# The normalized rows of a spectral block get a tile of their own: a third slot for the tag of the transfer tile

## The chip, the cores and the metric

The kernel runs on one core of one Trainium2 chip. The metric is the device time of one execution in microseconds (us), the median over several runs. Engines are named as the profile names them: PE (matrix products), PEld (its weight loads), DVE (VectorE), ACT (ScalarE), POOL (GpSimd) and SP, whose queue issues every DMA of this kernel ("SPq").

## The reference

Eight sequences x of 3136 rows and 256 channels pass through a spectral layer and then through a Fourier mixer with an MLP. Cut to what is computed:

```python
X = rfft(x, axis=1)
Yr = Xr @ w_r - Xi @ w_i + b_r
Yi = Xr @ w_i + Xi @ w_r + b_i
Y = soft(Yr) + 1j * soft(Yi)          # soft(v) = sign(v) * max(|v| - 0.01, 0)
y = irfft(Y, n=3136, axis=1)          # the "x" of the second part
u = y + real(fft(fft(y, axis=1), axis=2))
un = (u - mean(u)) / sqrt(var(u) + 1e-6)     # over the 256 channels
out = u + relu(un @ w_ch1) @ w_ch2    # 256 -> 1024 -> 256
```

## The kernel before, in words

A sequence of 3136 = 64 x 49 rows is transformed in two stages: first over the 64 (p1), then over the 49 with the twiddles in a table (p2_f2). p2_w mixes the channels and applies the soft threshold. From its result two things are made: the inverse transform (p2_yt transposes, p2_g2 does its first stage and stores it to the DRAM tensor bd), and the mixer's part, for which the spectrum is already there (p2_mix; its DVE, ACT and POOL steps end in the tile mq, stored to the DRAM tensor md). Most products are made in three terms of a high and a low part (mm3, lines L150, L151, L152); a tile ending in h is the high part and one ending in l the low part, and the lo helpers (L144 on DVE, L147 on POOL) make the latter.

The part around the change is p3, which runs over *pieces*: two of the 49 columns of a sequence at once, or one (there are 104 pieces, and 12 or 14 belong to a batch, that is a sequence; three or four columns make a group). For each piece:

- p3_norm loads a tile bf from bd (L669) and a tile mt from md (L673 and L675, three or six DMAs to a piece's rows), both from SP. ACT and POOL split bf into bh and bl, PE does the last stage of the inverse transform (g_g1), and DVE adds it to mt, which gives u in the tile ut (L683). DVE, ACT and POOL make mean and reciprocal deviation (L688 to L698), and L700 writes the normalized rows, **in place into mt**.
- p3_tr transposes them on PE (g_ut, L718); ACT and DVE make the two parts uth and utl.
- p3_mlp1 makes h = un @ w1 on PE in eight slices; ACT makes hh with the relu (L737) and DVE hl (L738). p3_mlp2 multiplies with w2 into o; DVE adds ut (L757) and SP stores the rows (L759).

Tiles come from a pool by tag. A tag has a number of slots (bufs), and a new tile takes the next one; the framework makes its first writer wait until all readers of the tile that held it are done. The tag of mt is also used by the split of the weights at the start (split_double, its tiles tf and r), by wi and by inv_f. The tile im (L445, L446) holds the imaginary part in one of the ways in which p2_f2 takes a result out of PSUM.

The order of the instructions on each engine is fixed when the program is built. Every step of each batch is a generator that yields a due time, and a heap takes the earliest; the pieces of p3 are due at

```python
yield t0 + T3 * (NRM + i / 4)      # p3_norm
yield t0 + T3 * (TR + i / 4)       # p3_tr
yield t0 + T3 * f / 8              # p3_mlp1
```

On top of that the framework orders the instructions with a time line of its own (`TileContext(nc, schedule_with_timeline_sim=True)`), in which an instruction is placed once its slots are there. So slots are handed out in the program's order, and a load whose slot is still held stands back in SP's row. At run time each engine's row is worked off from front to back. Other DMAs in SP's row are xf and ad (p1), af and tff (p2_f2's load and its table), tif (p2_yt's table), bd and md stores (L642; L565 to L579), and the stores to the output.

Of the kernel before, what the change touches and what calls it, by code (L numbers as in the profile page):

```python
# [10 lines left out]
F32 = mybir.dt.float32  # L11
# [8 lines left out]
D = 256  # L20
# [6 lines left out]
S = 50  # L27
# [101 lines left out]
def spectral_block(ctx: ExitStack, tc: tile.TileContext, x, w_ri, b_ri, w1, w2,  # L129
# [28 lines left out]
    def split_double(name, h, l, sl, src):  # L158
# [3 lines left out]
        def tmp(tag, bufs, dt=I32):  # L162
            return sb.tile([128, 512], dt, tag=tag, bufs=bufs, name=f"cv_{name}_{tag}")
# [3 lines left out]
        lo, hi = raw[:, 0::2], raw[:, 1::2]  # L167
        tf = tmp("mt", 2, F32)
        sc.activation(tf, hi.bitcast(F32), AF.Abs)
# [8 lines left out]
        va.tensor_scalar(e, w, -0x800000, None, op0=ALU.bitwise_and)  # L178
        r = tmp("mt", 2)
        va.tensor_scalar(r, lo, 8, None, op0=ALU.logical_shift_right)  # L180
# [24 lines left out]
    def load_consts():  # L205
        yield 0.97 * T
        behind("x", out=fwd_f, in_=c_fwd)
        w_v = w_ri.rearrange("a (k p) e -> a p k e", p=128)
        for name, tag in (("wr", "hh"), ("ws", "hh"), ("wd", "hl")):
            KF[name] = sb.tile([128, 2, D], F32, tag=tag, bufs=2, name=name + "f")  # L210
        behind("x", out=KF["wr"], in_=w_v[0])
        wi = sb.tile([128, 2, D], F32, tag="mt", bufs=2, name="wi")
        behind("x", out=wi, in_=w_v[1])

        for name, sign in (("ws", -1.0), ("wd", 1.0)):
            va.scalar_tensor_tensor(KF[name], wi, sign, KF["wr"], op0=ALU.mult, op1=ALU.subtract)
        for name in ("wr", "ws", "wd"):
            split(name, KF[name])
        yield 0.99 * T
        KF["cs"] = sb.tile([128, 2, 129], F32, tag="hl", bufs=2, name="csf")  # L220
        behind("x", out=KF["cs"], in_=c_cs)
        yield 1.55 * T
        split("fwd", fwd_f)

        cs = K["cs"] = cp.tile([128, 2, 2, 128], F32R, name="cs")
        t = KF["cs"]
        sc.copy(cs[:, :, 0], t[:, :, 0:128])
        lo_v(cs[:, :, 1], t[:, :, 0:128], cs[:, :, 0])
        sc.copy(cs[:, 0, 1, 0:1], t[:, 0, 128:129])
        inv = sb.tile([128, 128], F32, tag="mt", bufs=2, name="inv_f")  # L230
        nc.sync.dma_start(out=inv, in_=c_inv)
        split("inv", inv)
# [157 lines left out]
    def p2_f2(b):  # L390


        for q in range(4):
# [17 lines left out]
            for ui in range(4):  # L411
# [30 lines left out]
                else:  # L442
                    im = sb.tile([128, 2, 2, S], F32, tag="im", bufs=2, name="im")
                    put(sc.copy, [Xh], gv)
# [209 lines left out]
    def p3_norm(b):  # L654

        for gi, (g0, z) in enumerate(groups[b % 2]):
            t0, T3 = clock3(b, g0)
            for i, n in parts_of[z]:
# [7 lines left out]
                bf = sb.tile([128, 512], F32, tag="bf", bufs=2, name="bf")  # L666
                mt = sb.tile([128, 2, D], F32, tag="mt", bufs=2, name="mt")
                for r, (bb, n2) in enumerate(src):
# [28 lines left out]
                gp.tensor_scalar(vv[:, :n], vv[:, :n], -0.5, 1.5, op0=ALU.mult, op1=ALU.add)  # L697
                gp.tensor_mul(rs[:, :n], rs[:, :n], vv[:, :n])  # L698
                for j in range(n):
                    va.tensor_scalar(mt[:, j], ut[:, j], ag[:, j, 0:1], rs[:, j], op0=ALU.subtract, op1=ALU.mult)  # L700
                normed[b, gi, i] = mt
                uts[b, gi, i] = ut

    def p3_tr(b):
        for gi, (g0, z) in enumerate(groups[b % 2]):
            t0, T3 = clock3(b, g0)
            for i, n in parts_of[z]:
                yield t0 + T3 * (TR + i / 4)
                if i == 0:
                    uth = sb.tile([128, 2, 512], F32R, tag="uth", bufs=2, name="uth")  # L710
                    utl = sb.tile([128, 2, 512], F32R, tag="utl", bufs=2, name="utl")
                    uthl[b, gi] = uth, utl
                mt = normed.pop((b, gi, i))
                g = gtile("g_ut")
                gv = g.rearrange("p (k t) -> p k t", k=2)
                for j in range(n):
                    for k in range(2):
                        te.transpose(gv[:, k, j * 128:(j + 1) * 128], mt[:, j, k * 128:(k + 1) * 128], ident)  # L718
                tw = slice(i * 128, i * 128 + n * 128)
# [103 lines left out]
```

## Time and profile before

| | |
|---|---|
| median of 3 runs | 1958.12 us (1956.15 to 1961.05) |
| the profiled execution | 1961.45 us |
| its span, from first to last instruction | 1959.7 us |
| mean granted clock of PE | 0.969 |
| PE, PEld busy | 95%, 87% of the span |
| DVE, ACT, POOL busy | 67%, 44%, 36% |
| DMA | 233.05 MB, 119 GB/s |
| chain that ended last | PE 80%, DVE 7%, DMA 6%, SP's queue 3% |

The median is over unprofiled runs; every duration and wait in the text is from the one profiled execution. A timeline row gives start and length in us, engine, line, operation, tile written and tiles read, and in brackets how long the engine had been idle and what ended that. A row of a DMA on SPq shows how long SP took to issue it, not the transfer. A row of the view of waits reads: engine and line that waited, engine and line waited for, us in total, times, longest.

### The profile page before, as it was taken

To read this page: it belongs to the slowest core of one execution; us is meant where nothing else is said; L and a number is where in the kernel's file an instruction comes from. 1 tells how busy PE (TensorE), PEld (TensorE's weight loads), DVE (VectorE), ACT (ScalarE), POOL (GpSimd) and SP (SyncE) were. 2 spreads that over 40 slices of the span, in tenths; PEclk is the share of its full clock that TensorE was granted. 3 is DMA by queue.
4 is the path that set the end of the run, shared out by engine and by line. 5 is a ranking of instruction groups with operands and counts; after the bars stand their busy time and mean duration, and the time that the engine had idled before them with its cause. 6 is when DMAs were issued, how large, how long until landed. Compare 5 with 4: busy or idle time off the path is not lost.

```text
span 1959.7 us, 35047 instructions
## 1 busy us (share of the span) xinstructions
PE 1856.2 (95%) x12115; PEld 1709.1 (87%) x12115; DVE 1322.5 (67%) x2831; ACT 853.2 (44%) x1888; POOL 704.8 (36%) x1087
## 2 busy tenths in 40 slices
PE   4875799999999999999999999999999999999999
PEld 3764699989999999998999999998999998998999
DVE  2676677777776777766677777766777766675543
ACT  2443544444444454443444544434544434433322
POOL 0345544344433444343333443323543322322210
PEclk7886899999999999999999999999999999999999
DMA  7466654345443544434443444435433332223210
GB/s 215 122 177 192 154 139 131 101 119 148 115 122 109 152 129 121 117 98 138 136 134 104 136 137 114 127 99 141 136 106 98 107 98 89 83 70 109 68 41 25
DMA packets 163540, 233.05 MB, mean 119 GB/s; under 512 B 27484, under 2 KB 107428, under 8 KB 163364
## 3 DMA queue, kind: packets, MB, share of 16 engines
q1 hardware_dynamic: 163364, 230.82, 41.9%
q8 instruction: 97, 1.59, 0.3%
q14 instruction: 79, 0.65, 0.1%
HBM read 127.95 MB, written 102.76 MB: 118 GB/s over the span
## 4 chain that ended last, share of the span: by engine, by line
PE 80%; DVE 7%; DMA 6%; SPq 3%; issue 2%; ACT 1%; POOL 1%; DVEq 0%; POOLq 0%; ACTq 0%
PE o L150 8%; PE o L151 8%; PE o L152 8%; PE h L150 8%; PE h L151 8%; PE h L152 8%; PE g_f L419 4%; PE g_w L150 3%; PE g_w L152 3%; PE g_w L151 3%; PE g_g L150 2%; PE g_g L152 2%; PE g_g L151 2%; PE g_yt L609 2%; PE g_ut L718 2%
## 5 line engine op out<-in xcount | busy, mean ns | idle before, releaser
L151 PE MATMUL o<-w2h,hl 128*128 128x256 f32 x1568 | 431.4, 285 | 8.4 <-DVE hl L738 8.4
L738 DVE SCALAR_TENSOR_TENSOR hl<-h,hh 128x512 fp32r<-128x512 f32 (+1 forms) x416 | 272.3, 655 | 243.8 <-ACT hh L737 242.5
L737 ACT ACTIVATE hh<-h 128x512 fp32r<-128x512 f32 (+1 forms) x416 | 238.0, 573 | 443.0 <-PE h L152 382.7
L152 PE MATMUL o<-w2h,hh 128*128 128x256 f32 x1568 | 424.2, 280 | 0.0
L150 PE MATMUL o<-w2l,hh 128*128 128x256 f32 x1568 | 397.6, 286 | 2.5 <-DVE ut L757 2.3
L150 PE MATMUL h<-utl,w1h 128*128 128x512 f32 (+1 forms) x832 | 323.5, 389 | 8.1 <-DVE hl L738 8.1
L152 PE MATMUL h<-uth,w1h 128*128 128x512 f32 (+1 forms) x832 | 317.0, 381 | 0.0
L151 PE MATMUL h<-uth,w1l 128*128 128x512 f32 (+1 forms) x832 | 316.6, 381 | 0.0
L151 PEld LDWEIGHTS o<-w2h,hl 128*128 128x128 f32 x1568 | 297.3, 190 | 14.8 <-DVE hl L738 10.3
L152 PEld LDWEIGHTS o<-w2h,hh 128*128 128x128 f32 x1568 | 297.0, 189 | 3.2
L150 PEld LDWEIGHTS o<-w2l,hh 128*128 128x128 f32 x1568 | 286.3, 189 | 15.1 <-ACT Xsh L428 2.9
L147 POOL TENSOR_TENSOR bl<-bf,bh 128x512 fp32r<-128x512 f32 x104 | 130.0, 1251 | 298.3 <-ACT bh L678 296.1
L419 PE MATMUL g_f<-tff,af 98*128 98x100 f32 x1024 | 155.2, 284 | 25.8 <-DMA tff<-c_tf 13.0
L419 PEld LDWEIGHTS g_f<-tff,af 98*128 98x128 f32 x1024 | 148.5, 204 | 34.2 <-issue 23.4
L152 PEld LDWEIGHTS h<-uth,w1h 128*128 128x128 f32 x832 | 156.8, 189 | 23.8
L150 PEld LDWEIGHTS h<-utl,w1h 128*128 128x128 f32 x832 | 157.0, 189 | 22.8 <-DVE hl L738 9.0
L147 POOL TENSOR_TENSOR xl<-xf,xh 128x512 fp32r<-128x512 f32 (+1 forms) x75 | 97.1, 1295 | 203.2 <-ACT xh L362 201.3
L151 PEld LDWEIGHTS h<-uth,w1l 128*128 128x128 f32 x832 | 157.3, 189 | 13.4
L683 DVE TENSOR_TENSOR ut<-g_g,mt 128x512 f32<-128x512 f32 x104 | 68.3, 657 | 104.9 <-PE g_g L152 67.9
L147 POOL TENSOR_TENSOR Xl<-xx,Xh 128x400 fp32r<-128x400 f32 (+1 forms) x96 | 106.3, 1110 | 89.6 <-ACT Xh L428 69.3
L147 POOL TENSOR_TENSOR Xsl<-xs,Xsh 128x200 fp32r<-128x200 f32 x120 | 76.9, 642 | 161.4 <-ACT Xsh L428 144.2
L700 DVE TENSOR_SCALAR mt<-ut,ag,rs 128x256 f32<-128x256 f32 x196 | 90.8, 502 | 48.9 <-POOL rs L698 48.6
(155 smaller groups left out, 3811.3 us busy)
## 6 DMA issues: line engine op xcount, KB each, us to landing
bd<-bev SPq DMA_DIRECT2D x128, 196.0 KB
af<-ad SPq DMA_DIRECT2D x62, 392.0 KB
bf<-bd SPq DMA_DIRECT2D x184, 128.0 KB
out_dram<-ut SPq DMA_DIRECT2D x92, 256.0 KB
xf<-in_x SPq DMA_DIRECT2D x176, 128.0 KB
ad<-ev SPq DMA_DIRECT2D x168, 128.0 KB
md<-mq SPq DMA_DIRECT2D x112, 192.0 KB
mt<-md SPq DMA_DIRECT2D x416, 32.0 KB
```

The costliest lines, as they stand in the source:

```text
L147: gp.tensor_sub(out_, full, hi.bitcast(F32))
L150: te.matmul(o, lh, rl, start=start, stop=False)
L151: te.matmul(o, ll, rh, start=False, stop=False)
L152: return te.matmul(o, lh, rh, start=False, stop=stop)
L419: te.matmul(g[:, o:o + 100], afs[s][:, ui * D + k * 128:ui * D + k * 128 + 128], tfs[s][:, ui], start=True, stop=True)
L609: te.transpose(gt[:100, (v * 2 + o) * 128:(v * 2 + o + 1) * 128], y[:, o, place].rearrange("p c j -> p (c j)"), ident)
L683: va.tensor_add(ut[:, :n], g[:, :w].rearrange("p (n d) -> p n d", d=D), mt[:, :n])
L700: va.tensor_scalar(mt[:, j], ut[:, j], ag[:, j, 0:1], rs[:, j], op0=ALU.subtract, op1=ALU.mult)
L718: te.transpose(gv[:, k, j * 128:(j + 1) * 128], mt[:, j, k * 128:(k + 1) * 128], ident)
L737: sc.activation(hh[:, :w], h[:, :w], AF.Relu)
L738: va.scalar_tensor_tensor(hl[:, :w], h[:, :w], 0.0, hh[:, :w].bitcast(F32), op0=ALU.max, op1=ALU.subtract)
```

## The change

L700 writes into a new tile nm, which the transposes then read. nm has the tag of mt, and that tag gets three slots instead of two wherever it is used. The tag of im gives up one of its two slots, which frees the memory for that. From L699 on, lines have one more in the number afterwards (L718 is L719).

```diff
-        tf = tmp("mt", 2, F32)
+        tf = tmp("mt", 3, F32)
...
-        r = tmp("mt", 2)
+        r = tmp("mt", 3)
...
-                    im = sb.tile([128, 2, 2, S], F32, tag="im", bufs=2, name="im")
+                    im = sb.tile([128, 2, 2, S], F32, tag="im", bufs=1, name="im")
...
-                mt = sb.tile([128, 2, D], F32, tag="mt", bufs=2, name="mt")
+                mt = sb.tile([128, 2, D], F32, tag="mt", bufs=3, name="mt")
...
+                nm = sb.tile([128, 2, D], F32, tag="mt", bufs=3, name="nm")
                 for j in range(n):
-                    va.tensor_scalar(mt[:, j], ut[:, j], ag[:, j, 0:1], rs[:, j], op0=ALU.subtract, op1=ALU.mult)
-                normed[b, gi, i] = mt
+                    va.tensor_scalar(nm[:, j], ut[:, j], ag[:, j, 0:1], rs[:, j], op0=ALU.subtract, op1=ALU.mult)
+                normed[b, gi, i] = nm
...
-                mt = normed.pop((b, gi, i))
+                nm = normed.pop((b, gi, i))
...
-                        te.transpose(gv[:, k, j * 128:(j + 1) * 128], mt[:, j, k * 128:(k + 1) * 128], ident)
+                        te.transpose(gv[:, k, j * 128:(j + 1) * 128], nm[:, j, k * 128:(k + 1) * 128], ident)
```

Likewise, wi and inv_f ask for three slots of the tag.

Since slots are handed out in the program's order, the change also moves instructions. The numbers behind the names count the tiles and differ between the two programs by a few for the same tile; the number behind md, bd or ad is the batch, from 0.

SP's row where the second batch's pieces begin. mt_4456 (after: mt_4468) is the first piece's tile, mt_4693 (mt_4706) the second's, bf_4946 (bf_4960) the third's. Before:

```order
L675 DMA mt_4456<-md1_85 32x256 x2
L673 DMA mt_4693<-md1_85 32x512
L675 DMA mt_4693<-md1_85 32x256 x2
L759 DMA out_0_dram<-ut_3399 128x512
L369 DMA ad3_88<-ev_4548 64x2x256 x2
L759 DMA out_0_dram<-ut_3678 128x512
L673 DMA mt_4693<-md1_85 32x512
L675 DMA mt_4693<-md1_85 32x256
L642 DMA bd2_90<-bev_4596 98x512
L675 DMA mt_4693<-md1_85 32x256
L669 DMA bf_4946<-bd1_86 64x2x256 x2
```

After:

```order
L675 DMA mt_4468<-md1_85 32x256 x2
L669 DMA bf_4960<-bd1_86 64x2x256 x2
L760 DMA out_0_dram<-ut_3407 128x512
L669 DMA bf_5235<-bd1_86 64x2x256
L369 DMA ad3_88<-ev_4561 64x2x256 x2
L760 DMA out_0_dram<-ut_3687 128x512
L262 DMA xf_5147<-in_x 64x512
L642 DMA bd2_90<-bev_4609 98x512
L262 DMA xf_5147<-in_x 64x512
L669 DMA bf_5235<-bd1_86 64x2x256
L669 DMA bf_5468<-bd1_86 64x2x256 x2
L673 DMA mt_4706<-md1_85 32x512
```

The second piece's six loads, which followed the first's, now stand behind the bf loads of the next three pieces, two stores of the output and the stores of ad and bd.

SP's row at the fourth-last piece of the same batch (mt_6816, after: mt_6838) and the md stores of batch 2. Before:

```order
L759 DMA out_0_dram<-ut_5470 128x512
L673 DMA mt_6816<-md1_85 32x512
L675 DMA mt_6816<-md1_85 32x256 x2
L759 DMA out_0_dram<-ut_5723 128x512
L673 DMA mt_6816<-md1_85 32x512
L675 DMA mt_6816<-md1_85 32x256 x2
L669 DMA bf_7427<-bd0_84 64x256
L669 DMA bf_7427<-bd1_86 64x256
L565 DMA md2_89<-mq_5874 24x2x1024
```

After:

```order
L669 DMA bf_7452<-bd0_84 64x256
L669 DMA bf_7452<-bd1_86 64x256
L565 DMA md2_89<-mq_5892 24x2x1024
L566 DMA md2_89<-mq_5892 2x1x1024
L567 DMA md2_89<-mq_5892 24x2x1024
L577 DMA md2_89<-mq_5892 24x2x1024
L578 DMA md2_89<-mq_5892 2x1x1024
L579 DMA md2_89<-mq_5892 24x2x1024
L673 DMA mt_6838<-md1_85 32x512
L675 DMA mt_6838<-md1_85 32x256 x2
L673 DMA mt_6838<-md1_85 32x512
L675 DMA mt_6838<-md1_85 32x256 x2
```

The piece's loads have moved behind two bf loads and the six md stores.

DVE's row at the first piece of the last batch: ut_22579 (after: ut_22669) is the sum that L683 makes from this piece's mt, hl_22558 (hl_22648) a slice of the MLP of an earlier group. Before:

```order
L738 SCALAR_TENSOR_TENSOR hl_22535<-h_22527,hh_22534 128x512
L738 SCALAR_TENSOR_TENSOR hl_22558<-h_22550,hh_22557 128x512
L683 TENSOR_TENSOR ut_22579<-g_g1_22575,mt_22562 128x512
L688 BN_STATS st_22581<-ut_22579 128x6 x2
L689 BN_AGGR ag_22582<-st_22581 128x2 x2
```

After:

```order
L739 SCALAR_TENSOR_TENSOR hl_22625<-h_22617,hh_22624 128x512
L683 TENSOR_TENSOR ut_22669<-g_g1_22665,mt_22652 128x512
L739 SCALAR_TENSOR_TENSOR hl_22648<-h_22640,hh_22647 128x512
L688 BN_STATS st_22671<-ut_22669 128x6 x2
L689 BN_AGGR ag_22672<-st_22671 128x2 x2
```

The add and that hl have changed places.

More of the change, by code (lines that the diff above doesn't have):

```diff
@@ L211, in load_consts @@
         behind("x", out=KF["wr"], in_=w_v[0])
-        wi = sb.tile([128, 2, D], F32, tag="mt", bufs=2, name="wi")
+        wi = sb.tile([128, 2, D], F32, tag="mt", bufs=3, name="wi")
         behind("x", out=wi, in_=w_v[1])
@@ L229, in load_consts @@
         sc.copy(cs[:, 0, 1, 0:1], t[:, 0, 128:129])
-        inv = sb.tile([128, 128], F32, tag="mt", bufs=2, name="inv_f")
+        inv = sb.tile([128, 128], F32, tag="mt", bufs=3, name="inv_f")
         nc.sync.dma_start(out=inv, in_=c_inv)
```

## The prediction, made before the changed kernel was run

> **What bounds the kernel now.** I read the page first, then busy time by stage, then who waits for whom on PE, on SP's DMA queue and on DVE, and last the timeline where those waits lie. The page and the table by stage (columns: stretch, its length, then busy time and count of PE, PEld, DVE, ACT and POOL, granted clock, DMA share, GB/s):
>
> ```profile
> PE 1856.2 (95%) x12115; PEld 1709.1 (87%) x12115; DVE 1322.5 (67%) x2831; ACT 853.2 (44%) x1888; POOL 704.8 (36%) x1087
> ...
> 0.00:225.00 225.00, 146.35 (x628) 116.97 (x629) 124.40 (x237) 88.99 (x213) 79.97 (x96) 0.76 0.62 174
> ...
> 300.00:1900.00 1600.00, 1579.51 (x10584) 1467.98 (x10583) 1114.23 (x2418) 708.66 (x1554) 585.56 (x930) 1.00 0.40 113
> ```
>
> PE is the bound: from 300 to 1900 us it is busy 1579.51 of 1600 us at the full granted clock of 1.00. Whatever the change does there can win 20.5 us at most. The first 225 us hold 78.6 us without PE work, so that part hangs on chains of transfers and of the other engines. What PE waits for in the long stretch (total us, times, longest):
>
> ```profile
> PE o L151 <- DVE hl L738: 8.4, 10, 2.8
> PE h L150 <- DVE hl L738: 8.1, 2, 4.8
> PE o L150 <- DVE ut L757: 2.3, 2, 1.4
> PE g_ut L718 <- DVE mt L700: 1.2, 3, 0.7
> ```
>
> PE nearly never waits for the normalized rows (1.2 us). It waits for hl, a DVE step of the MLP. The same view for SP's queue and for DVE:
>
> ```profile
> SPq L673 <- PE g_ut L718: 130.4, 50, 6.0
> SPq L673 <- DVE mt L700: 44.2, 20, 6.0
> ...
> DVE hl L738 <- ACT hh L737: 212.2, 185, 4.6
> DVE ut L683 <- PE g_g L152: 66.1, 42, 4.4
> DVE ut L683 <- DMA mt<-md: 21.8, 8, 6.0
> ```
>
> SP stands 130.4 us before the load of mt until the transposes of an earlier piece have read the slot. But the add that uses the load (L683) waits for it only 8 times. Those 8 lie where a batch begins, and there is the link from mt to PE:
>
> ```profile
> 884.21 0.69 DVE L683 TENSOR_TENSOR ut<-g_g,mt 128x512 f32<-128x512 f32 x1 [5.15 <-DMA mt<-md]
> ...
> 887.50 0.50 PE L150 MATMUL h<-utl,w1h 128*128 128x512 f32 x1 [3.36 <-DVE hl L738]
> ...
> 1343.46 0.69 DVE L683 TENSOR_TENSOR ut<-g_g,mt 128x512 f32<-128x512 f32 x1 [6.03 <-DMA mt<-md]
> ...
> 1346.75 0.79 PE L150 MATMUL h<-utl,w1h 128*128 128x512 f32 x1 [4.75 <-DVE hl L738]
> ...
> 1112.14 0.69 DVE L683 TENSOR_TENSOR ut<-g_g,mt 128x512 f32<-128x512 f32 x1 [2.73 <-DMA mt<-md]
> ```
>
> The add stands in DVE's row ahead of hl, so while it waits for the transfer hl waits too: 5.15 us of waiting became 3.36 of idle PE and 6.03 became 4.75, while 2.73 us became none. So this kernel forgives about 1.3 to 2.7 us of a late mt.
>
> **The change, part by part.** *Instructions.* None is added and none removed: L700 writes into nm instead of mt and L718 reads nm, with the same shapes. Cost 0, on either side.
>
> *What the slots do.* Before, the tag has two addresses, so the load of piece i+1 takes the slot of piece i-1 and waits for its transposes. After, three addresses go round in program order mt, nm, mt, nm: the load of piece i+1 gets the address of nm of piece i-1, which the same transposes read. The wait for PE is the same one, and the tile "that no DMA writes" lies where a DMA wrote two allocations earlier. What differs is the place in line: nm of piece i now asks for its slot between the two loads, and the loads of piece i+1 stand some nine DMA instructions later in SP's row, the others ahead of them some four earlier.
>
> *Steady pieces.* Here is piece 17, the last two of its six loads and the add:
>
> ```profile
> 488.21 0.83 SPq L675 DMA_DIRECT2D mt<-md x2
> ...
> 513.30 0.69 DVE L683 TENSOR_TENSOR ut<-g_g,mt 128x512 f32<-128x512 f32 x1
> ```
>
> The load is out 24.3 us ahead of its use. Nine instructions cost by this row 0.42 us each, 3.7 us, if none waits; if one or two wait like the longest in SP's list (6.0), 10 to 16. Cost 0, covered by the 24 us; if that cover were gone, each late load would cost as at the batch beginnings.
>
> *Batch beginnings.* The first piece's load hangs on the md stores, which stay where they were, so the two large gaps above stay. DVE's row around 884 and 1343 is the same in both programs. The second piece's load moves behind bf loads, stores and ad stores. At the second batch:
>
> ```profile
> 424.48 0.88 SPq L675 DMA_DIRECT2D mt<-md x2
> 425.46 0.36 SPq L673 DMA_DIRECT2D mt<-md x1
> ...
> 439.46 1.24 SPq L669 DMA_DIRECT2D bf<-bd x2
> ...
> 426.81 0.69 DVE L683 TENSOR_TENSOR ut<-g_g,mt 128x512 f32<-128x512 f32 x1 [1.51 <-DMA mt<-md]
> ...
> 441.05 0.69 DVE L683 TENSOR_TENSOR ut<-g_g,mt 128x512 f32<-128x512 f32 x1
> ```
>
> The first piece shows the transfer: issue over at 425.36, add at 426.81, 1.45 us. The second piece's load, at 425.46 before, now stands behind the bf load that was at 439.46. If that one keeps its time, mt goes out from 440.7 to 443.4, lands at 444.9 and the add is 3.8 us late. If only the order counts, the ten instructions ahead take some 6 us and it lands near 436, in time. The bf load waits for the bl step two pieces back, whose own bf load now leaves earlier (it stood behind mt), so I take the second: 0, with 3.8 - 2.7 = 1.1 to 3.8 - 1.3 = 2.5 us as the upper end.
>
> *The fourth-last piece of batches 1, 3 and 5.* There the load stood ahead of the bf load and the md stores of the next part; now it stands behind them:
>
> ```profile
> 591.21 0.49 SPq L579 DMA_DIRECT2D md<-mq x1
> ...
> 593.59 0.68 DVE L683 TENSOR_TENSOR ut<-g_g,mt 128x512 f32<-128x512 f32 x1
> ```
>
> Six loads of some 0.45 us from 591.7 end at 594.4 and land at 595.9, 2.3 us after the add's old time. By the pairs above that is 0 to 1 us of PE each; I take 0.33 each, +1.0 for three, bounds 0 and 3.
>
> *The last batch's first piece.* On DVE the add is moved ahead of an hl:
>
> ```profile
> 1775.89 0.69 DVE L738 SCALAR_TENSOR_TENSOR hl<-h,hh 128x512 fp32r<-128x512 f32 x1 [4.61 <-ACT hh L737]
> 1778.36 0.69 DVE L683 TENSOR_TENSOR ut<-g_g,mt 128x512 f32<-128x512 f32 x1 [1.78 <-DMA mt<-md]
> ...
> 1776.64 0.39 PE L151 MATMUL o<-w2h,hl 128*128 128x256 f32 x1 [0.23 <-DVE hl L738]
> ...
> 1780.69 0.39 PE L151 MATMUL o<-w2h,hl 128*128 128x256 f32 x1 [1.03 <-DVE hl L738]
> ```
>
> If mt lands as before, that hl comes 3.16 us later (1779.05 for 1775.89) and PE with it; the idle 1.03 us after it is then covered: +2.1. But on ACT the mq copy L558, which leads to md and so to this mt, is moved ahead of the cast of bf that waited 1.33 us:
>
> ```profile
> 1765.95 0.62 ACT L678 CAST bh<-bf 128x512 fp32r<-128x512 f32 x1 [1.33 <-DMA bf<-bd]
> ...
> 1766.95 0.62 ACT L558 COPY mq<-mq 100x508 f32<-100x508 f32 x1
> ```
>
> Two ACT steps of 0.6 us less make mt 1.2 us sooner, with the wait 2.3 us. I take +1.0 of the 2.1, bounds 0 and 2.1. The other beginnings trade one hl of 0.7 us each way: 0, bounds -1 and +1.
>
> *The first batch.*
>
> ```profile
> 181.63 0.16 DVE L551 TENSOR_TENSOR mq<-g_mix,mq 100x1 f32<-100x1 f32 x1 [7.06 <-ACT mq L545]
> ...
> 183.17 1.10 DVE L144 TENSOR_TENSOR til<-tif,tih 100x392 fp32r<-100x392 f32 x1 [0.72 <-ACT tih L602]
> ...
> 201.00 0.42 SPq L673 DMA_DIRECT2D mt<-md x1
> ...
> 211.89 0.69 DVE L683 TENSOR_TENSOR ut<-g_g,mt 128x512 f32<-128x512 f32 x1 [0.59 <-DMA bf<-bd]
> ...
> 208.63 0.66 PE L718 MATMUL g_ut<-ident,mt 128*128 128x128 f32 x2 [12.01 <-DVE mt L700]
> ```
>
> The til step now stands ahead of L551, on the chain that ends in PE's wait of 12.01 us: 0 to 1.1 us, I take 1.0. The second piece's load moves from 201.00 behind ten others, at 0.6 us each to 207, and lands at 211.3 for an add at 211.89: 0, upper end 2.
>
> *The im tile, two slots to one.*
>
> ```profile
> L445 ACT COPY im<-g_f x36: 328/342/359, 37.8 to 1691.9; 128x200 f32<-128x200 f32 x36
> ...
> L446 DVE TENSOR_TENSOR xs<-g_f,im x36: 353/367/369, 38.3 to 1692.3; 128x200 f32<-128x200 f32 x36
> ...
>   DVE xs L446: 3.4, 6
> ```
>
> A copy now waits until the add before it has read the slot. 36 copies in 1654 us are 46 us apart on average and the first and the last add start 0.4 to 0.5 us after their copies, so 0; were each copy held up by an add's length, that would be 36 x 0.367 = 13.2 us on ACT, which is idle 56% of the time. The Trainium skill ("Trainium Kernel Development and Optimization", Best Practices) says to double-buffer so that transfer and compute overlap, which speaks against one slot. By it the 13.2 us would stand on the path and the sum would be 1974. Here im is filled by ACT and not by a DMA, and DVE waited for it six times only.
>
> **The sum.** 1.0 (first batch) + 1.0 (three late pieces) + 1.0 (last batch) = +3. The profiled execution took 1961.45 us, of which 1959.7 are the span and 1.75 lie around it; it is 3.3 us above the median of the runs, so I add the 3 to the median: 1958.1 + 3 = 1961. Differences under 0.3%, 5.9 us, can't be told from no change here: 1952.2 to 1964.0 counts as the same.
>
> **The rivals.**
>
> *Late second pieces: slower.* At the beginnings of batches 1 to 7 the moved load lands after the add's turn, DVE holds hl back and PE stands. For it: the 3.8 us worked out at 441; two of the present waits already cost PE 3.36 and 4.75. Against it: bf loads leave earlier. From 2.7 us late on it costs. With 3.8 us late at seven beginnings, 1.1 to 2.5 us each, 8 to 17, it gives 1958 + 12 = 1970.
>
> *SP set free: faster.* The 130.4 us of SP's waits go or shrink, bf, xf and md move ahead, and the gaps at beginnings close. For it: rows that stood behind mt move up. Against it: both large gaps hang on the transfer of the first piece after md, not on a slot. If the 3.36, 4.75 and 2.8 went, 10.9 us: 1947; half is likelier, 1951. The limit is 20.5, 1938. A rule of the Trainium skill ("Perfetto Trace Analysis", Optimization Strategy) leads here: the same gap repeated on the engine that should be full can mean too few buffers. The trace shows no such series on PE, 20 us in 17 unlike waits.
>
> *im's single slot.* Each of the 36 copies is held up by an add and PE by each copy: 13.2 us as worked out above, 1961 + 13 = 1974. Against it: their distance of 46 us.
>
> *Nothing happens.* The wait is the same and the moved rows are all covered: 1958, within the bound.
>
> **How the numbers follow.** My sum of small losses 0.46, nothing happens 0.17, late second pieces 0.24 (of which 0.05 stay inside the bound), SP set free 0.11 (0.02 inside), im's single slot on the path 0.02. Same: 0.46 less 0.04 that go over the bound, + 0.17 + 0.05 + 0.02 = 0.66. Slower 0.19 + 0.04 + 0.02 = 0.25, faster 0.09. The likeliest case's own range is 1956 to 1965 (bounds: losses 0 and 8). To leave out no more than 2 in 10 it reaches down to half of the faster rival, 1951, and up to the middle of the slower one, 1970.
>
> **What would show it.** After: the wait of L673 for g_ut stays or turns into a wait of other rows for the same time; PE's busy time stays at 1856; the gaps near 887 and 1347 stay. Late pieces would show as more than 8 waits of L683 for mt and more idle PE before hl. I am wrong if PE idles much more or less than 20.5 us from 300 to 1900, or if the first 225 us change by more than 3.

## The result and the profile after

The changed kernel is slower. Its median over four runs is 1980.72 us (1979.51 to 1983.91), beside 1957.13 us (1954.13 to 1961.05) for four runs of the kernel before. The ratio of the two means is 1.0122, with an interval from 1.0100 to 1.0144: about 23.6 us lost, where 3 were forecast. (All ratios below are such ratios of means, each to runs of the kernel before on the same chip; so they differ a little from a quotient of medians.) The profiled execution took 1983.91 us with a span of 1982.1 us, at a mean granted clock of 0.969 as before.

The busy line of the page after, and the table by stage with the same columns as before:

```profile
PE 1869.6 (94%) x12115; PEld 1719.6 (87%) x12115; DVE 1321.9 (67%) x2831; ACT 851.0 (43%) x1888; POOL 703.5 (35%) x1087
...
0.00:225.00 225.00, 141.28 (x610) 111.76 (x611) 120.38 (x232) 87.33 (x210) 78.58 (x94) 0.76 0.62 172
...
300.00:1900.00 1600.00, 1575.23 (x10466) 1463.28 (x10466) 1104.95 (x2402) 701.66 (x1545) 582.16 (x921) 0.99 0.40 113
1900.00:1982.10 82.10, 78.15 (x543) 75.65 (x541) 35.15 (x75) 20.19 (x43) 4.57 (x21) 0.99 0.10 35
```

Every engine does the same number of instructions as before. Yet PE is busy for 1869.6 us instead of 1856.2: 13.4 of the 22.4 us by which the span grew are *longer products*, and only 9.0 are idle time (112.5 instead of 103.5 us, span less busy). In the long stretch PE is idle for 24.8 us, 4.3 more than before, and does 10466 products in the time in which it did 10584.

Which products became longer is in the groups of the page (count | busy, mean ns of one | idle before). First the kernel before, then after:

```profile
L151 PE MATMUL o<-w2h,hl 128*128 128x256 f32 x1568 | 431.4, 285 | 8.4 <-DVE hl L738 8.4
L152 PE MATMUL o<-w2h,hh 128*128 128x256 f32 x1568 | 424.2, 280 | 0.0
L150 PE MATMUL o<-w2l,hh 128*128 128x256 f32 x1568 | 397.6, 286 | 2.5 <-DVE ut L757 2.3
```

```profile
L151 PE MATMUL o<-w2h,hl 128*128 128x256 f32 x1568 | 436.7, 287 | 5.9 <-DVE hl L739 5.8
L152 PE MATMUL o<-w2h,hh 128*128 128x256 f32 x1568 | 429.7, 283 | 0.0
L150 PE MATMUL o<-w2l,hh 128*128 128x256 f32 x1568 | 400.3, 288 | 7.4 <-ACT hh L738 7.3
```

The three groups of the second MLP product hold 5.3, 5.5 and 2.7 us more, 13.5 together, as much as all of the additional busy time (the three groups of h hold 3.3 more, others less). Neither their tiles nor their lines are touched by the diff.

The waits of the long stretch: one of SP's queue before, then PE, SP's queue and DVE after.

```profile
SPq L669 <- POOL bl L147: 80.0, 26, 9.6
```

```profile
PE h L150 <- DVE hl L739: 8.7, 4, 4.0
PE o L150 <- ACT hh L738: 7.3, 7, 4.1
PE o L151 <- DVE hl L739: 5.8, 8, 1.5
...
SPq L669 <- POOL bl L147: 137.5, 35, 9.6
...
DVE ut L683 <- DMA mt<-md: 34.2, 9, 6.0
```

SP's 130.4 us of waiting for the transposes are gone from the list, and its wait for the bf slots has grown from 80.0 to 137.5 us: one wait took the place of the other. DVE's add waits 34.2 us for mt instead of 21.8, in nine pieces instead of eight. PE's wait for hh (7.3 us) is new. Most of it is the beginning of batch 1, here on DVE, ACT and PE:

```profile
434.49 0.69 DVE L683 TENSOR_TENSOR ut<-g_g,mt 128x512 f32<-128x512 f32 x1 [4.70 <-DMA mt<-md]
...
436.50 0.62 ACT L678 CAST bh<-bf 128x512 fp32r<-128x512 f32 x1 [4.99 <-DMA bf<-bd]
437.03 0.52 ACT L428 CAST Xh<-xx 128x400 fp32r<-128x400 f32 x1
437.45 0.59 ACT L738 ACTIVATE hh<-h 128x512 fp32r<-128x512 f32 x1
...
438.09 0.80 PE L150 MATMUL o<-w2l,hh 128*128 128x256 f32 x2 [4.06 <-ACT hh L738]
...
439.63 0.41 PE L151 MATMUL o<-w2h,hl 128*128 128x256 f32 x1
439.84 0.41 PE L152 MATMUL o<-w2h,hh 128*128 128x256 f32 x1
...
443.27 0.28 PE L152 MATMUL o<-w2h,hh 128*128 128x256 f32 x1
443.39 0.28 PE L151 MATMUL o<-w2h,hl 128*128 128x256 f32 x1
```

The add waited 4.70 us for mt (before: 1.51 at 426.81). On ACT the cast of the third piece's bf, which before stood behind three of these relus, now stands ahead of them and waits 4.99 us, so PE stands for 4.06. And the wait costs more than its length: o products then start 0.21 us apart until 441, and 0.12 us apart at 443. Two stages of 5 us there and the stretch of the slow products, PE alone (length, busy, count, granted clock):

```profile
435.00:440.00 5.00, 1.91 (x7) 0.78 0.79 242
438.10:441.00 2.90, 2.90 (x12) 0.50 0.83 251
440.00:445.00 5.00, 5.00 (x30) 0.88 0.62 189
```

### The profile page after: what moved, and what is told of

It reads as the page before. It is cut to its first block, busy times and chain, and to the rows that moved or that the text cites. A ratio compares the mean times of both kernels' runs of the same rounds, so it can differ in the third digit from the quotient of the medians.

```text
span 1982.1 us, 34689 instructions
## 1 busy us (share of the span) xinstructions
PE 1869.6 (94%) x12115; PEld 1719.6 (87%) x12115; DVE 1321.9 (67%) x2831; ACT 851.0 (43%) x1888; POOL 703.5 (35%) x1087
## 4 chain that ended last, share of the span: by engine, by line
PE 81%; DVE 7%; DMA 6%; SPq 3%; issue 2%; ACT 1%; POOL 1%; DVEq 0%; POOLq 0%; ACTq 0%
PE o L151 9%; PE o L150 8%; PE o L152 8%; PE h L150 8%; PE h L152 8%; PE h L151 8%; PE g_f L419 4%; PE g_w L150 3%; PE g_w L152 3%; PE g_w L151 3%; PE g_g L150 2%; PE g_g L152 2%; PE g_g L151 2%; PE g_yt L609 2%; PE g_ut L719 2%
## 5 line engine op out<-in xcount | busy, mean ns | idle before, releaser
L151 PE MATMUL o<-w2h,hl 128*128 128x256 f32 x1568 | 436.7, 287 | 5.9 <-DVE hl L739 5.8
L152 PE MATMUL o<-w2h,hh 128*128 128x256 f32 x1568 | 429.7, 283 | 0.0
L683 DVE TENSOR_TENSOR ut<-g_g,mt 128x512 f32<-128x512 f32 x104 | 68.3, 656 | 121.7 <-PE g_g L152 73.0
L701 DVE TENSOR_SCALAR nm<-ut,ag,rs 128x256 f32<-128x256 f32 x196 | 88.9, 492 | 55.8 <-POOL rs L698 55.5
```

What stands on the lines that cost most here:

```text
L151: te.matmul(o, ll, rh, start=False, stop=False)
L152: return te.matmul(o, lh, rh, start=False, stop=stop)
L683: va.tensor_add(ut[:, :n], g[:, :w].rearrange("p (n d) -> p n d", d=D), mt[:, :n])
L701: va.tensor_scalar(nm[:, j], ut[:, j], ag[:, j, 0:1], rs[:, j], op0=ALU.subtract, op1=ALU.mult)
```

## The experiments

The theories after the first look: (1) the tiles behind the tag of mt moved in memory, and that makes o's products longer; (2) loads and casts at the batch beginnings come at a worse time, through the order; (3) the single slot of im; (4) a separate tile, or a third slot, costs by itself.

How a stretch compares in two kernels is worked out thus: the start of PE's n-th product in one trace less the start of PE's n-th product in the trace of before, and the growth of that difference from the first to the last product of the stretch. The products are numbered in order of start, 12115 in each kernel.

**Placement alone.** In the built programs w2h begins at byte 193440 of its partition before and at 194688 after: the tag of mt grew by 2048 bytes, that of im shrank by 800. hh stays at 100064. Divided by 64 bytes, w2h's place leaves the remainder 32 before and 0 after; hh's leaves 32 in both. This kernel takes the one before and lengthens each of the three slots of tff, so that the tiles behind them, w2 among them, move by the same 1248 bytes. The order on all engines is that of before.

```diff
-                tff = sb.tile([98, 4, 100], F32, tag="tff", bufs=3, name="tff")
+                tff = sb.tile([98, 504], F32, tag="tff", bufs=3, name="tff")[:, :400].rearrange("p (u t) -> p u t", u=4)
```

> The kernel before with one edit: each of the three slots of tff is 416 bytes longer than it needs to be, so every tile behind it, the weights w2 among them, lies 1248 bytes further on, where the changed kernel has it. All engines' rows are those of the kernel before. Theory A (place in memory): in the changed kernel the o products start 119 ns after one another instead of 117 (median), all through the span, and only they read a tile that was shifted (w2) against one that was not (hh, hl). 4704 of them by about 2.4 ns are 11 us, so this kernel takes about 1957 + 10 = 1967 us and shows 119 ns. Rival (another run, another chip): 117 ns stay and the time is 1957.

Measured: 1966.46 us (1955.22 to 1973.87), ratio 1.0057 [1.0037, 1.0077]. The same instructions in the same order cost 0.57% more, so placement does it. Products 6600 and 7930 bound a stretch in which PE is never idle. First before, then this kernel:

```profile
1121.80 0.37 PE L150 MATMUL o<-w2l,hh 128*128 128x256 f32 x1
...
1321.41 0.28 PE L151 MATMUL o<-w2h,hl 128*128 128x256 f32 x1
```

```profile
1126.72 0.36 PE L150 MATMUL o<-w2l,hh 128*128 128x256 f32 x1
...
1327.34 0.28 PE L151 MATMUL o<-w2h,hl 128*128 128x256 f32 x1
```

199.61 us before, 200.62 here: 1.0 us in 200 without any wait.

**The changed kernel, 32 bytes on.** 32 unused bytes behind im give w2h the remainder 32 again. The order is that of the changed kernel.

```diff
-                    im = sb.tile([128, 2, 2, S], F32, tag="im", bufs=1, name="im")
+                    im = sb.tile([128, 208], F32, tag="im", bufs=1, name="im")[:, :200].rearrange("p (k s t) -> p k s t", k=2, s=2)
```

> The changed kernel with 32 unused bytes behind im, so that w2 and all that follows lie 1280 bytes further on than before the change instead of 1248: again at 32 from a multiple of 64 bytes. All engines' rows are those of the changed kernel. Theory A as a matter of alignment: the o products are back at 117 ns and some 9 us of the 23.6 are gone: ratio about 1.0075, 1969 to 1973 us. If the distance counts and not the alignment: 119 ns and 1981. What is left at 117 ns is the price of the moved rows.

Measured: 1966.87 us (1964.77 to 1976.11), 1.0057 [1.0036, 1.0078]. 32 bytes take 1.0122 to 1.0057. The same two products, first after, then this kernel, and its groups of o:

```profile
1144.05 0.36 PE L150 MATMUL o<-w2l,hh 128*128 128x256 f32 x1
...
1344.63 0.28 PE L151 MATMUL o<-w2h,hl 128*128 128x256 f32 x1
```

```profile
1130.57 0.37 PE L150 MATMUL o<-w2l,hh 128*128 128x256 f32 x1
...
1330.15 0.28 PE L151 MATMUL o<-w2h,hl 128*128 128x256 f32 x1
...
L151 PE MATMUL o<-w2h,hl 128*128 128x256 f32 x1568 | 431.3, 285 | 4.5 <-DVE hl L739 4.3
L152 PE MATMUL o<-w2h,hh 128*128 128x256 f32 x1568 | 424.0, 280 | 0.0
L150 PE MATMUL o<-w2l,hh 128*128 128x256 f32 x1568 | 395.9, 285 | 8.3 <-ACT hh L738 8.2
```

200.58 us became 199.58, and the groups are back at the values of before. The median distance between the starts of o products that follow each other directly (300 to 1900 us, from the trace) is 117 ns before and here, 119 ns after and in the kernel above. 2 ns on 3 x 1568 products are 9.4 us, most of the 0.57 to 0.65% (11 to 13 us) between the members of these pairs (by the mean distances, 116.0 and 118.4 ns without the slow stretches, 11.3 us).

**A single slot for im, nothing else.** The kernel before, with one slot of double length, so that no address changes.

```diff
-                    im = sb.tile([128, 2, 2, S], F32, tag="im", bufs=2, name="im")
+                    im = sb.tile([128, 400], F32, tag="im", bufs=1, name="im")[:, :200].rearrange("p (k s t) -> p k s t", k=2, s=2)
```

> The kernel before with im on one slot of twice the length, so that every other tile stays where it was. ACT's and DVE's rows change in a few places of the first batch only. Theory A (the place of w2): the o products start 117 ns after one another as in the kernel before, since w2 has not moved, and the time is that of the kernel before, 1954 to 1958 us. Rival 1 (the chip or the run makes the 119 ns): 119 ns here too. Rival 2 (the single im slot costs, up to the 13 us of the forecast): 117 ns and up to 1970.

Measured: 1959.36 us, 1.0005 [0.9989, 1.0022], 117 ns. im's second slot is worth nothing here; theory 3 falls.

**All tiles 32 bytes on.** The kernel before with 32 bytes ahead of every other tile. If an absolute remainder counted, this would cost what placement cost above.

```diff
+    pad = cp.tile([128, 8], F32, name="pad")
+    va.memset(pad[:, 0:1], 0.0)
```

> The kernel before with one tile of 32 bytes ahead of all others (and one memset of it at the start): every tile lies 32 bytes further on, so the weights w2 and w1 and also hh, hl, uth and utl are at a multiple of 64. All rows are those of the kernel before. If what counts is that the two tiles that a product reads agree in alignment, the o products stay at 117 ns and the time at 1954 to 1958 us. If the tile that is streamed through has to be off the multiple of 64 (or w2 for itself), o goes to 119 ns, and h perhaps by as much: 1963 to 1970 us.

Measured: 1956.52 us, 1.0001 [0.9988, 1.0014], 117 ns, with both w2h (193472) and hh (100096) at the remainder 0. So it's not where the tiles lie by itself, but whether they agree.

**Which tiles must agree.** The kernel before with 32 more bytes in Xh, which lies ahead of hh, hl and w2 but not of w1, uth and utl: the operands of o move, those of h stay.

```diff
+        Xh = sb.tile([128, 1608], F32R, tag="Xh", bufs=1, name="Xh")
+        Xh = Xh[:, :1600].rearrange("p (k u c j) -> p k u c j", k=2, u=8, c=2)
...
```

> The kernel before with the tile Xh 32 bytes longer: hh, hl and w2 move by 32 bytes together, to a multiple of 64, while w1, uth and utl stay at 32 from it. A few rows change places (30 of 1890 on ACT, 63 of 11516 on PE). If what counts for the o products is that the two tiles they read (hh or hl, and w2) agree, o stays at 117 ns and the time near 1956. If w2 has to agree with the tiles of the h products, which run between the o products, o and h go to 119 and 231 ns, and the time to 1966.

Measured: 1956.71 us, 0.9986 [0.9974, 0.9998], 117 ns. With hh, hl and w2 moved together nothing is lost: the remainder of w2 against that of hh and hl is what counts, not that against the tiles of the first MLP product. The 0.14% gained are under what can be told from no change.

**The new tile in the tag of its own.** The changed kernel with one slot of an own tag for nm, mt at two slots, im at one. Now the transposes no longer hold a load, which was the rival "SP set free".

```diff
-                mt = sb.tile([128, 2, D], F32, tag="mt", bufs=3, name="mt")
+                mt = sb.tile([128, 2, D], F32, tag="mt", bufs=2, name="mt")
...
-                nm = sb.tile([128, 2, D], F32, tag="mt", bufs=3, name="nm")
+                nm = sb.tile([128, 2, D], F32, tag="nm", bufs=1, name="nm")
```

> nm gets a tag of its own with one slot, mt goes back to two, im keeps one: the load of the next piece no longer waits for transposes. bh stands on ACT's row as before the change at all three beginnings. Theory B: none of the three steps is there. With theory A, w2 lies 800 bytes lower than before, again at another remainder of 64, so 119 ns: 1957 + 10 = 1967; without A 1957. If freeing the load from the transposes were worth something, it would be below these by up to the 20 us that PE idles.

Measured: 1966.47 us, 1.0058 [1.0037, 1.0080], 119 ns; w2h lies at 192640, remainder 0. The same kernel with the 32 bytes behind im (192672, remainder 32):

> The kernel with a tag of its own for nm (one slot, mt two, im one), with 32 unused bytes behind im so that w2 lies at 32 from a multiple of 64 again; all rows as in the kernel without them, which took 1966.5 us at 119 ns. Theory A: 117 ns and 9 us less, 1957 us, ratio 1.001 +- 0.002. If theory A is wrong, 1966.

Measured: 1957.85 us, 1.0006 [0.9991, 1.0021], 117 ns. So a tile of its own for the normalized rows costs nothing once the remainders agree. It brings nothing either: that loads no longer wait for transposes is worth nothing to this kernel.

**Three slots without a new tile.** The changed kernel with L700 in place as before, the tag still at three slots, im at one.

```diff
-                nm = sb.tile([128, 2, D], F32, tag="mt", bufs=3, name="nm")
...
-                    va.tensor_scalar(nm[:, j], ut[:, j], ag[:, j, 0:1], rs[:, j], op0=ALU.subtract, op1=ALU.mult)
-                normed[b, gi, i] = nm
+                    va.tensor_scalar(mt[:, j], ut[:, j], ag[:, j, 0:1], rs[:, j], op0=ALU.subtract, op1=ALU.mult)
+                normed[b, gi, i] = mt
```

> Three slots for the tag of mt and one for im as in the changed kernel, but no nm: the rows are normalized in place. Addresses are those of the changed kernel. bh stands as before the change at all three beginnings. Theory B: no steps. Theory A: 119 ns and 1967 us; without A 1957. Rival (the third slot or the single im slot is what costs): 1981.

Measured: 1973.52 us (1965.85 to 1975.06), 1.0084 [1.0056, 1.0112], 119 ns. And with the 32 bytes behind im:

> Three slots for the tag of mt, rows normalized in place, one im slot, and 32 unused bytes behind im, so that w2 is aligned with hh again; the same kernel without them took 1973.5 us (ratio 1.0084) at 119 ns. By theory A 0.57% of that goes: ratio 1.0027, 1961 us, at 117 ns. If its loss had another cause, 1973.

Measured: 1965.69 us (1960.23 to 1969.33), 1.0025 [1.0010, 1.0041], 117 ns. The third slot itself costs a quarter of a per cent, 5 us; placement is the rest, for the third time (0.59%, after 0.65% and 0.52%).

**The slot of nm taken early.** In the changed kernel nm is allotted at L700, between the loads of two pieces. Here it is allotted with mt and claimed by a small write, so that mt always gets the same slot and nm one of the two others.

```diff
                 mt = sb.tile([128, 2, D], F32, tag="mt", bufs=3, name="mt")
+                nm = sb.tile([128, 2, D], F32, tag="mt", bufs=3, name="nm")
+                gp.memset(nm[:, 0, 0:1], 0.0)
...
-                nm = sb.tile([128, 2, D], F32, tag="mt", bufs=3, name="nm")
```

> The changed kernel, but POOL clears one element per partition of nm right after the piece's loads are issued, so that nm takes its slot there and not at L701; three slots, nm and one im slot stay. On ACT's row the cast bh of the pieces 28 and 54 (the third of batches 2 and 4) then stands where it stood before the change, that of piece 14 (batch 1) stays where the change put it. Theory B (order at the beginnings): the changed kernel's PE falls back by 4.9, 4.8 and 3.7 us at the beginnings of batches 1, 2 and 4 because the casts of bf are in another place among the relus; here the first of the three stays and the other two go: 1981 - 8.5 = 1972 us, plus up to 2 for 104 small POOL steps. Rival (the slots or the tile itself): all three stay, 1981.

Measured: 1973.79 us, 1.0086 [1.0058, 1.0114], 119 ns: as much as three slots in place (1.0084). So 0.36% of the change seem to hang on *when* nm asks for its slot, through the rows that move with it. The two intervals, [1.0100, 1.0144] and [1.0058, 1.0114], overlap a little, and the next table shows that what is left is not the same loss in both kernels.

Where the parts lie can be read, as far as single executions show it, from the growth of PE's lag behind the kernel before, in us, one profiled execution each (columns by the time in before):

| kernel | to 259 | 415 to 632, batch 1 | 632 to 664, batch 2 begins | 664 to 865, no idle PE | 1122 to 1321, no idle PE |
|---|---|---|---|---|---|
| after | 3.53 | 7.82 | 3.83 | 0.93 | 0.97 |
| after, 32 bytes | 0.65 | 6.85 | 3.26 | 0.01 | -0.03 |
| slot of nm early | 0.09 | 7.71 | 1.21 | 0.98 | 1.01 |
| three slots in place | 3.32 | 3.35 | 0.92 | 1.00 | 1.07 |
| the same, 32 bytes | 5.86 | 2.36 | 0.14 | 0.04 | 0.00 |
| own tag, 32 bytes | -2.56 | 4.57 | 0.29 | -0.06 | -0.02 |
| im single | -2.13 | 2.05 | 0.47 | 0.00 | -0.04 |
| all 32 bytes on | -4.21 | 2.06 | 0.64 | 0.04 | -0.04 |

The last two columns are placement: about 1.0 in each kernel whose remainders differ, and between -0.06 and 0.04 where they agree. (The kernel with the longer Xh, whose rows on PE have changed places, shows 0.33 and 0.29 at 117 ns.) The last two rows are kernels as fast as before, so the profiled execution of before was some 2 us lucky at batch 1. With nm in the shared tag 4.5 us more are lost at batch 1 and 3.1 at batch 2 than with three slots in place (second row against the fifth). The early claim takes back those at batch 2 (1.21, where the changed kernel has 3.83), but not those at batch 1 (7.71 and 7.82); it lost less to 259 us instead. And the own tag, as fast as before over its ten runs, shows 4.57 at batch 1 in its profile, the slowest of the ten. So the loss at batch 1 isn't shown to hang on the moment of the slot, and single profiles don't tell where the 0.36% lie. The new order also wins: at the beginning of batch 6 (1547 to 1588 us) the lag falls by 3.0 us after and by 2.8 with the 32 bytes, by 0.0 with im single and 0.1 with all 32 bytes on.

**The cast of bf held back.** Is it the early cast in ACT's row, or the late mt in DVE's, that costs at batch 1? In the changed kernel with the 32 bytes the cast of that piece is kept behind the hh that it stood behind before.

```diff
+                late = {(1, 4): (0, 5, 2)}.get((b, m))
+                if late:
+                    with tc.issue_after(hh_ins[late]):
+                        sc.copy(bh[:, :w], bf[:, :w])
...
```

> The changed kernel with w2 aligned again (32 unused bytes behind im; that alone took 1966.9 us, ratio 1.0057) and one row put back: on ACT the cast bh of piece 14, the third of batch 1, is held until the relu hh of the third slice of batch 0's last group, where it stood before the change; all SP rows but a few stay. Theory B (the cast waits for its bf and holds the relus behind it): the 4.06 us of idle PE near 438 go to about 1.9, which the kernels with the old rows show there too, and with it the slow clock behind it: 4 to 5 us less, about 1962, ratio 1.003. Rival (the late mt, for which DVE's add waits 4.7 us there, is what costs): the idle time stays, because hl waits behind the add, 1967.

Measured: 1967.36 us (1959.02 to 1969.42), 1.0050 [1.0031, 1.0069], beside 1.0057 without it. PE at the beginning of batch 1, first without, then with the cast held back:

```profile
434.50 0.50 PE L150 MATMUL o<-w2l,hh 128*128 128x256 f32 x2 [3.71 <-ACT hh L738]
```

```profile
434.09 0.39 PE L150 MATMUL o<-w2l,hh 128*128 128x256 f32 x1 [1.20 <-DVE ut L764]
436.35 0.39 PE L151 MATMUL o<-w2h,hl 128*128 128x256 f32 x1 [1.86 <-DVE hl L745]
```

The wait for hh is gone, and waits for ut and hl, both on DVE behind the add, stand in its place: 3.06 instead of 3.71 us. The cast was only the first of two things that were late together; the late mt alone does nearly as much. Not all of that is the change's: with im single PE stands 3.0 us from 415 to 450 us, in the order of before.

**Two more casts held back,** at the beginnings of batches 2 and 4.

```diff
-                late = {(1, 4): (0, 5, 2)}.get((b, m))
+                late = {(1, 4): (0, 5, 2), (2, 4): (1, 5, 5), (4, 4): (3, 5, 5)}.get((b, m))
```

> As the kernel with one cast put back, and the casts bh of pieces 28 and 54 (third of batches 2 and 4) are held until the relu of the sixth slice of the group before, some ten ACT rows later than the change left them. Theory B: ACT's waits for bf of 3.6 to 4.5 us at the beginnings of batches 2 and 4 go too, and PE's idle time there falls to that of the kernels with the old rows: 2 to 4 us less again, about 1959, ratio 1.001. Rival: no change against the kernel with one cast put back, 1962 or 1967.

Measured: 1968.10 us, 1.0055 [1.0034, 1.0077]: no gain, a miss. At batch 2 PE now stands 2.72 us for hl:

```profile
663.41 0.38 PE L151 MATMUL o<-w2h,hl 128*128 128x256 f32 x1 [2.72 <-DVE hl L745]
```

**The first batch.** The kernels with three slots have PE waiting longer for af near 180 us. PE's row in before stands in the prediction (3.63 us); here after, and three slots in place with the 32 bytes:

```profile
180.00 1.15 PE L419 MATMUL g_f<-tff,af 98*128 98x100 f32 x4 [7.44 <-DMA af<-ad]
```

```profile
181.31 1.15 PE L419 MATMUL g_f<-tff,af 98*128 98x100 f32 x4 [7.05 <-DMA af<-ad]
```

In SP's row two stores of ad stand ahead of these loads that stood behind them before. Put back by a due time, on the changed kernel with the 32 bytes and on three slots in place with them:

```diff
-            yield T * (t0 + width * ci / len(todo))
+            yield T * (t0 + width * ci / len(todo) + 0.02 * ((b, ci) == (2, 1)))
```

> The changed kernel with w2 aligned (that alone: ratio 1.0057) and one due time put back by 0.02 of a batch: the second chunk of batch 2 in p1. In SP's row its two stores of ad then stand behind the first loads of af, as before the change, and not ahead of them; of all other rows some five per engine change. Theory C (the first batch): with the third slot these stores, which wait for DVE's ev, stand ahead of the af loads, PE waits 7.1 to 7.4 us for af near 180 instead of 2.4 to 3.6, and PE is 6 us later at 209 than in the kernels with two slots. Here the wait for af falls to about 3 and 3 to 6 us go: ratio about 1.0035, 1963 us. Rival (something else in the first batch, such as the weights' split with three slots): 7 us of wait stay, ratio 1.0057.

> The kernel with three slots, rows in place and w2 aligned (ratio 1.0025) with the same due time put back. Its beginnings of later batches cost what those of the kernel before cost. Theory C: its whole loss is in the first batch, so ratio 1.000 +- 0.0015. Rival: 1.0025.

Measured: 1962.93 us, 1.0036 [1.0020, 1.0051] on the first (1.0057 without), and 1962.90 us, 1.0026 [1.0013, 1.0039] on the second (1.0025 without). The first number is as forecast, but the mechanism isn't there; the wait stays in both:

```profile
174.52 1.15 PE L419 MATMUL g_f<-tff,af 98*128 98x100 f32 x4 [6.94 <-DMA af<-ad]
```

```profile
177.65 1.15 PE L419 MATMUL g_f<-tff,af 98*128 98x100 f32 x4 [7.86 <-DMA af<-ad]
```

So the order of these stores isn't the cause of the wait. In the profiles the lag at 259 us does fall by some 6 us in both (-5.0 instead of 0.65, 0.1 instead of 5.86), but only the first kernel's time fell with it, and its interval overlaps that of the kernel without: that stays unexplained. Without these two kernels, the lag at 259 us lies between -7.5 and 0 in the profiles of seven kernels with two slots (mean -3.0, before itself among them) and between 0.1 and 5.9 in seven with three (mean 2.4). The 5.4 us between the means are about what the third slot costs (0.25% are 5 us). That it is lost in the first batch is so far only this comparison of single profiles. Whether a third slot makes af late at all is open too: with the stores put back the first of the two kernels begins this product at 174.52 us, earlier than before (177.48), although PE had waited longer for it.

## Why the prediction was wrong

*The step that failed most:* "None is added and none removed: L700 writes into nm instead of mt and L718 reads nm, with the same shapes. Cost 0, on either side." The instructions are the same; their operands are not where they were. A change in the number of slots moved w2 by 1248 bytes against hh and hl, and 4704 products of a kernel that PE bounds became 2 ns longer. This is 0.52 to 0.65% of the 1.22%, shown by four pairs of kernels that differ in a pad alone. The prediction had no term for addresses and wrote that "PE's busy time stays at 1856"; that line was the right one to look at, and it went to 1869.6. With 32 bytes the changed kernel takes 1966.87 us, inside the range of 1951 to 1970: the missing term is what put the result out of it. Of its other tests, idle PE from 300 to 1900 rose by only 4.3 us and would have said little; the first 225 us did change by more than 3 (busy 141.28 instead of 146.35 us).

*Batch beginnings.* Taken at 0, for the second pieces. From batch 1 on these were indeed in time. The first piece's add at batch 1 came 7.7 us later than before, but that doesn't refute "The first piece's load hangs on the md stores, which stay where they were": PE itself was 3.8 us behind at 415 us, and the copy of mq ahead of the md stores took 2.5 us longer, as it did in kernels with the order of before (last section). That leaves some 1.4 us. What the prediction didn't look at here is ACT's row: the cast of the third piece's bf had moved ahead of three relus, waited for its load and held back hh. With that cast held back, the wait for DVE's add, the mechanism that the prediction did name, cost nearly as much. From 415 to 450 us PE stood 5.1 us, beside 3.0 with im single and 1.0 before, and after the longest of these gaps the clock was slow for 3.4 us. By the table the changed kernel with the 32 bytes lost 4.8 us more than im single at batch 1 and 2.8 at batch 2, where the rival "late second pieces" had 1.1 to 2.5 at each beginning. How much of that hangs on the moment at which nm takes its slot stays open.

*The pairs of wait and idle time.* Of the 8 waits of L683 for mt in the kernel before, seven lie where a batch begins; the eighth, 0.49 us at 1537.54, doesn't. And "this kernel forgives about 1.3 to 2.7 us of a late mt" counts idle time alone. The clock behind a gap wasn't counted, though the kernel before shows it too: after the gap of 3.36 us at 887,

```profile
890.00:895.00 5.00, 5.00 (x38) 0.78 0.76 230
```

PE was fully busy at a granted clock of 0.78. On the other side more can be forgiven than that, as the three late pieces below show.

*The first batch.* Taken at 1.0, by the til step ahead of L551. PE's wait for the normalized rows, where that would show, is 11.54 us instead of 12.01. But it is 8.77 to 10.73 in three kernels with the order of before, so single profiles show no cost of that step and can't rule one out. The second piece's load, held to be just in time, came a little late: its add waited 1.00 us for mt, and PE 2.04 us for its rows (1.37 before, without a releaser in the profile). The third slot costs about 5 us; that they are lost in the first batch is argued from the lags above.

*The three late pieces and the last batch,* 1.0 each. The adds of all three pieces did come to wait:

```profile
609.28 0.69 DVE L683 TENSOR_TENSOR ut<-g_g,mt 128x512 f32<-128x512 f32 x1 [3.99 <-DMA mt<-md]
...
1074.10 0.69 DVE L683 TENSOR_TENSOR ut<-g_g,mt 128x512 f32<-128x512 f32 x1 [3.25 <-DMA mt<-md]
...
1538.51 0.69 DVE L683 TENSOR_TENSOR ut<-g_g,mt 128x512 f32<-128x512 f32 x1 [3.33 <-DMA mt<-md]
```

PE had no idle time around them (585 to 640, 1066 to 1090, 1530 to 1558 us): late as foreseen, at no price, although these waits are longer than the 1.3 to 2.7 us that were held to be forgiven. From 1588 to 1790 us by the time of before, where the last batch begins, PE's idle time grew by 0.16 us, where 1.0 was taken. The add that had moved ahead of hl came at 1797.34; less the 20.3 us that PE was behind at 1760, that is 1.4 us sooner than before (1778.36), much as foreseen (1.2). It waited 5.17 us, with hl behind it, and PE stood 1.35 us for that hl.

*Right:* the wait for the transposes wasn't loosened but taken over by others in SP's row, and setting SP free is worth nothing (own tag, 1.0006). The two large gaps stayed: 3.96 and 3.51 us instead of 3.36 and 4.75.

```profile
904.59 0.51 PE L150 MATMUL h<-utl,w1h 128*128 128x512 f32 x1 [3.96 <-DVE hl L739]
...
1368.96 0.50 PE L150 MATMUL h<-utl,w1h 128*128 128x512 f32 x1 [3.51 <-DVE hl L739]
```

And im: DVE waited for it 3.4 us in six times before, and

```profile
  DVE xs L446: 3.5, 6
```

after, with 1.0005 for the slot alone. The double-buffer rule weighed in the prediction (the Trainium skill, "Trainium Kernel Development and Optimization", Best Practices) doesn't bite on a tile that ACT fills once in 46 us.

The parts of the 1.22%: placement 0.52 to 0.65, from four pairs; the third slot 0.25, from two kernels; and 0.3 to 0.36 that go when nm takes its slot early or the rows are normalized in place. This last part is the least certain: with only one due time moved the kernel with the 32 bytes came down from 1.0057 to 1.0036. None of the kernels tried is clearly faster than the one before.

## What to carry to other kernels

A change in the number or size of buffers is also a change of every address behind them: where an engine is the bound, compare the mean duration of its largest groups before looking for waits, and run the same program with a pad of 32 bytes before blaming the order. A shared rotating tag ties a tile's load to the moment at which another tile asks for its slot; a tag of its own for the second kind of tile undid that here at no cost. A gap on PE can cost more than its length, by the slow clock behind it.

## What the runs showed of the hardware

- The o products of 256 columns follow each other every 117 ns when w2 and hh or hl have the same remainder by 64 bytes (32 and 32, 0 and 0), and every 119 ns at 0 and 32 (w2 at 0, hh and hl at 32; medians; by group 116 to 117 and 118 to 119), in all 16 kernels. The reverse, w2 at 32 and hh and hl at 0, and other remainders weren't tried, and why it is so is open. The Trainium skill ("TensorE: Matmul & The Clock Gate", section "Wait — 56ns, not 53.3ns?") gives the distance, measured there with bf16, as columns by 2.4 GHz and a fixed 2.5 ns, an estimate of 109 ns for 256 columns. These runs show 117 for products in fp32r with a weight load each, and an addition that depends on where the operands lie.
- After a gap PE can work at a lower granted clock: 0.50 from 437.8 to 441.2 us, at the end of the gap of 4.06 us and behind it, with 0.21 us from one o product to the next. By the same section of the Trainium skill a cold array takes columns by 1.2 GHz, an estimate of 213 ns, and that agrees. From 300 to 1900 us, in the 16 profiles together, all 23 gaps of over 3.3 us had such a stretch behind them, 3.4 or 6.8 us long from its start; of the 50 gaps of 1.4 to 3.3 us 26 had one. At the same place in batch 1, a gap of 1.86 us had one in the own tag with the 32 bytes and a gap of 1.87 us none with im single.
- The copy of mq at L559 took 1.53 us in the profiled execution of before and 4.02 us after, and 4.02 too where the order was that of before:

```profile
414.36 1.53 DVE L559 COPY mq<-mq 100x508 f32<-100x508 f32 x1 [0.16 <-POOL mq L556]
```

```profile
418.06 4.02 DVE L559 COPY mq<-mq 100x508 f32<-100x508 f32 x1 [0.49 <-POOL mq L556]
```

It is part of why the profile of before was ahead of its equals at batch 1. What the length goes with is in POOL's row. In the 16 profiles 199 of these copies have no POOL instruction beside them, and all take 0.41 to 0.43 us. The copy of 4.02 us ends at 422.08, behind a run of POOL's splits of which this one ends at 421.79:

```profile
420.53 1.26 POOL L147 TENSOR_TENSOR xl<-xf,xh 128x512 fp32r<-128x512 f32 x1
```

In the profile of before the copy ends at 415.89, while the next split of that run, which began at 415.57, is 1.73 us long instead of 1.28. So the two seem to hold each other up; which one gets ahead in an execution is open.
